# Turning q and k of six batches by VectorE squares and DMA instead of TensorE, in a fused attention and feed-forward kernel

## Chip, cores and metric

One core of a Trainium2 chip (trn2). The metric is device time in microseconds (us) of one execution; lower is better. Every comparison below takes a kernel's fast runs against runs of the kernel before on the same chip in the same rounds. All profiles are of one execution each.

## The reference, cut to what matters

```python
# q, k, v: (8 batches, 8 heads, 576 positions, 64)
scores = scale * np.matmul(q, k.transpose(0, 1, 3, 2))          # scale = 1/8
scores = np.where((rel >= 0) & (rel < 128), scores + bias, -1e9) # ALiBi, window of 128
attn = softmax(scores)
x = (attn @ v).transpose(0, 2, 1, 3).reshape(4608, 512)
h = x @ w_in                                                    # 512 -> 2048
out = np.where(h > 0, h, np.exp(np.minimum(h, 0)) - 1) @ w_out  # 2048 -> 512, ELU
```

For `q @ k.T` TensorE needs q and k with the 64 head dimensions on the partitions, so both have to be turned. The feed-forward part needs x with its 512 features on the partitions, so x is turned as well (tile `xT`).

## The kernel before

The kernel is a list of some 160 steps. Tasks are put into steps by hand with `at(step, f, args)`; each engine executes its own share in the order in which it was issued. Batch b has its attention in steps 16b to 16b+15, the feed-forward part runs beside it. The parts that matter here (cuts are marked `# ...`):

```python
XBAR = 2
QK = [one([128, H, 2, 640], F16, f"QK{i}") for i in range(2)]   # rows 0-63 data, 64-127 bias terms

def load_qk(b, w, h0=0, h1=H):                 # software queue, f32 to f16, 512 KB
    # ...
    nc.gpsimd.dma_start(stq[b][:, w, h0:h1, :, :]..., (q, k)[w][b, h0:h1, 0:512, :]...)

def transposes(b, hp):                         # two heads, q and k, on TensorE
    t = ps_s.tile([128, 2, 2, 4, 2, 32], F16, name="tp", tag="sps")   # the scores' PSUM ring, 2 buffers
    for g in range(2):
        for w in (1, 0):
            for j in range(2):
                nc.tensor.transpose(t[:, g, w, :, j, :], stq[b][...], ident)
    for odd in range(2):                       # evicted by ScalarE (odd hp) or VectorE
        # ...
        if hp % 2: nc.scalar.copy(o, i)
        else:      V.tensor_copy(o, i)

def turn(b, i):                                # x of one block -> xT
    if b >= XBAR:                              # batches 2..7: DMA transpose on SyncE's queue
        # ...
        nc.sync.dma_start_transpose(out=xT[:, :, o:o + n], in_=x[0:n, :])
        return
    # batches 0 and 1: four TensorE transposes into PSUM, one VectorE copy
    # ...

def hidden(t, j):                              # h = x @ w_in for 128x512, then exp and min
    p = hps[t, j] = ps_h.tile([128, 512], F32, name="hp", tag="hp")   # 2 buffers
    # ... nc.tensor.matmul(p[...], w_in_sb[...], xT[...])
    nc.scalar.activation(e, p, AF.Exp)
    nc.gpsimd.tensor_scalar(out=e, in0=e, scalar1=1.0, scalar2=0.0, op0=ALU.min, op1=ALU.max)
# elu(): one VectorE instruction (g) one step later; only it frees the hp buffer

def fill(i):                                   # bias terms, by DMA
    nc.sync.dma_start(QK[i][64:128, :, 0, 0:576], TQ[64:128, :].unsqueeze(1).broadcast_to([64, H, 576]))
    nc.sync.dma_start(QK[i][g_, :, 1, :], TK[g_, :].unsqueeze(1).broadcast_to([32, H, 640]))
# ...
at(s0 + ((5, 9, 10, 13) if b > 1 else ...)[hp], transposes, b + 1, hp)
at(s0 + 10 + 2 * i, load_qk, b + 2, w)         # for b >= 1
```

A hidden block of tokens can start only when their x has landed in `xT`. For batches 2 and 3 that is three steps after `turn`, for batches 4 to 7 seven or more.

The softmax here doesn't subtract the row's maximum and nothing guards it: scores larger than these inputs give would overflow.

Of the kernel before, what the change touches and what calls it, by code (L numbers as in the profile page):

```python
# [9 lines left out]
F16 = mybir.dt.float16  # L10
# [9 lines left out]
def kernel(  # L20
# [9 lines left out]
    nc = tc.nc  # L30
# [34 lines left out]

    QK = [one([128, H, 2, 640], F16, f"QK{i}") for i in range(2)]
    VP = [one([128, 5, H, VW], F16, f"VP{i}") for i in range(2)]
# [5 lines left out]

    stq, stt, vf, vs = {}, {}, {}, {}

# [73 lines left out]
    with tc.manual_schedule():  # L149
# [68 lines left out]
        def zeros():  # L218
            for i in range(2):
                V.memset(QK[i][0:64 + 64 * i, :, 1, 576:640], 0.0)  # L220
                V.memset(VP[i][64:128, 4, :, 0:D], 0.0)
            for e in EX:
                V.memset(e[:, 512:576], 0.0)
# [4 lines left out]
        is96, is97, isx = small("is96"), small("is97"), small("isx")  # L228
        TQ = one([128, 576], F16, "TQ")
        TK = one([128, 640], F16, "TK")  # L230
# [12 lines left out]
        def terms():  # L243

            V.tensor_scalar(out=is96, in0=rowf, scalar1=96.0, scalar2=None, op0=ALU.is_equal)
            V.tensor_scalar(out=is97, in0=rowf, scalar1=97.0, scalar2=None, op0=ALU.is_equal)
            V.tensor_scalar(out=isx, in0=is97, scalar1=-1.0, scalar2=None, op0=ALU.mult)
            V.tensor_scalar(out=pm[r_, :], in0=posi[r_, :], scalar1=float(-MID), scalar2=None,
                            op0=ALU.add)
            V.tensor_scalar(out=TQ[r_, :], in0=pm[r_, :], scalar1=isx[r_, :], scalar2=is96[r_, :],  # L250
                            op0=ALU.mult, op1=ALU.add)
            V.tensor_scalar(out=TK[r_, 0:576], in0=pm[r_, :], scalar1=is96[r_, :],
                            scalar2=is97[r_, :], op0=ALU.mult, op1=ALU.add)
            V.memset(TK[64:128, 576:640], 0.0)

# [8 lines left out]

        def fill(i):
            nc.sync.dma_start(QK[i][64:128, :, 0, 0:576],
                              TQ[64:128, :].unsqueeze(1).broadcast_to([64, H, 576]))
            nc.sync.dma_start(QK[i][g_, :, 1, :], TK[g_, :].unsqueeze(1).broadcast_to([32, H, 640]))

        def fill_k(i):  # L270
            nc.sync.dma_start(QK[i][r_, :, 1, :], QK[1 - i][r_, :, 1, :])

        def k_term(h):
            V.tensor_scalar(out=QK[1][r_, h, 1, :], in0=TK[r_, :],
                            scalar1=8.0 * 2.0 ** (-8.0 * (h + 1) / H), scalar2=None, op0=ALU.mult)

        zeros()
# [8 lines left out]
        def transposes_half(a, hq):  # L286

            if a:
                t = ps_o.tile([128, 4, 2, 2, 2, 32], F16, name="tph", tag="op")
            else:  # L290
                t = ps_s.tile([128, 4, 2, 2, 2, 32], F16, name="tp", tag="sps")
            p = slice(64 * a, 64 * a + 64)
            for w in (1, 0):
                for g in range(4):
                    for j in range(2):
                        nc.tensor.transpose(
                            t[:, g, w, :, j, :],
                            stq[0][p, w, 4 * hq + g, 2 * j:2 * j + 2, :].rearrange("p a d -> p (a d)"),
                            ident[p, p])
            for odd in range(2):  # L300
                r = slice(64 * odd, 64 * odd + 64)
                o = QK[0][0:64, 4 * hq:4 * hq + 4, :, 256 * a:256 * a + 256].rearrange(
                    "p h w (m o i) -> p (h w) m o i", o=2, i=32)[:, :, :, odd, :]
                i = t[r, :, :, :, :, :].rearrange("p h w n a i -> p (h w) (n a) i")
                (nc.scalar.copy if hq else V.tensor_copy)(o, i)

        def transposes(b, hp):
            t = ps_s.tile([128, 2, 2, 4, 2, 32], F16, name="tp", tag="sps")
            for g in range(2):
                for w in (1, 0):  # L310
                    for j in range(2):
                        nc.tensor.transpose(  # L312
                            t[:, g, w, :, j, :],
                            stq[b][:, w, 2 * hp + g, 2 * j:2 * j + 2, :].rearrange("p a d -> p (a d)"),
                            ident)
            for odd in range(2):
                r = slice(64 * odd, 64 * odd + 64)
                o = QK[b % 2][0:64, 2 * hp:2 * hp + 2, :, 0:512].rearrange(
                    "p h w (n a i) -> p (h w) n a i", a=2, i=32)[:, :, :, odd, :]
                i = t[r, :, :, :, :, :].rearrange("p h w n a i -> p (h w) (n a) i")  # L320
                if hp % 2:
                    nc.scalar.copy(o, i)  # L322
                else:
                    V.tensor_copy(o, i)  # L324

        def transposes_tail(b):
            t = ps_s.tile([128, NP, 2, 64], F16, name="tpt", tag="sps")
            for hp in range(NP):
                for w in range(2):
                    nc.tensor.transpose(  # L330
                        t[:, hp, w, :],
                        stt[b][:, w, 2 * hp:2 * hp + 2, :].rearrange("p h d -> p (h d)"),
                        ident[0:64, 0:64])
            for g in range(2):
                r = slice(64 * g, 64 * g + 64)
                V.tensor_copy(
                    QK[b % 2][0:64, :, :, 512:576].rearrange("p (n g) w c -> p n g w c", g=2)[:, :, g, :, :],
                    t[r, :, :, :])

        def scores(b, s):  # L340
# [6 lines left out]
            def mm(o, h, kc, qc, n):  # L347
                nc.tensor.matmul(t[:, o:o + n], qk[0:r, h, 1, kc:kc + 128], qk[0:r, h, 0, qc:qc + n],  # L348
                                 start=b > 0 or o == 0, stop=b > 0)
# [5 lines left out]
            elif i < 4:  # L355
                hs = [2 * p, 2 * p + 1]
                for l in range(2):
                    mm(256 * l, hs[l], 128 * i, 128 * i, 128)
                    mm(256 * l + 128, hs[l], 128 * i - 128, 128 * i, 128)
            else:  # L360
                hs = [4 * p + l for l in range(4)]
                for l in range(4):
                    mm(128 * l, hs[l], 384, 512, 64)
                    mm(128 * l + 64, hs[l], 512, 512, 64)
            if b == 0:
# [161 lines left out]
        for b in range(B):  # L527
# [16 lines left out]
            if b + 1 < B:  # L544
                for hp in range(NP):
                    at(s0 + ((5, 9, 10, 13) if b > 1 else (9, 10, 13, 14) if b else (14, 14, 15, 15))[hp],
                       transposes, b + 1, hp)
                at(s0 + (14 if b else 25), transposes_tail, b + 1)
# [16 lines left out]
        at(9, group_rows)  # L565
        at(10, fill, 1)
        at(10, bands)
        for h in range(H):
            at(11 + h // 2, k_term, h)
        at(22, fill, 0)  # L570
        at(22, fill_k, 0)
        at(9, load_wo, 2, 1)
# [55 lines left out]
```

## Time and profile before

| | |
|---|---|
| time, median of 4 runs | 367.09 us (366.05 to 368.67) |
| TensorE, VectorE, ScalarE, GpSimd busy | 94%, 67%, 57%, 40% |
| one batch of attention in the middle (16 steps) | 36.77 us |
| the same 16 steps with nothing left to turn | 33.69 us |
| moved by DMA | 37.1 MB |

The lines behind it are in the prediction. How to read them: PE is TensorE, PEld its weight loads, DVE VectorE, ACT ScalarE, POOL GpSimd and SP SyncE; L451 is line 451 of the program. A group line has the line of the program, engine, operation, output and input with shapes, the count, then busy us and mean ns of one, then the idle time of the engine just before and what ended it. A chain line has start and length in us. The main instrument of this document is a table of step times: the start of each step's first `hp` matmul, taken from the timeline of TensorE. Where the text says that a step took so long, it is the time from that start in the step before to that start in the step.

### The profile page before, as it was taken

The page shows a single profiled execution, that of the slowest core. Times are in us where ns is not written, and L with a number is a line of the kernel's source. Part 1 is how long each engine was busy: PE and PEld are TensorE (multiplying, and loading weights), DVE is VectorE, ACT ScalarE, POOL GpSimd, SP SyncE. Part 2 cuts the span into 40 slices and gives each one's busy share as a digit, 9 for nine tenths or more (in the row PEclk, how much of TensorE's full clock was granted, in tenths as well). Part 3 has the DMA queues.
Part 4 walks back from the last instruction along what each step waited for, and adds up shares of the span by engine and source line. Part 5 has one row for each costly group of instructions (what it writes and reads, how often), then busy time and mean ns, then how long its engine had stood idle before and what let it go on. Part 6 is the DMA issues. An engine that isn't in the chain of part 4 may idle for free.

```text
span 363.7 us, 9613 instructions
## 1 busy us (share of the span) xinstructions
PE 340.3 (94%) x3790; PEld 251.6 (69%) x3790; DVE 243.5 (67%) x574; ACT 206.7 (57%) x349; POOL 145.7 (40%) x229
## 2 busy tenths in 40 slices
PE   6878997999979999989999999999999999999994
PEld 6766775777647667767777777777777777666651
DVE  6479889678886776666676767776776756634430
ACT  4355583666537655765566665666567565543431
POOL 9146623434314723472346334642433232233320
PEclk9899999999999999999999999999999999999999
DMA  8999999839243973497448934793631222211113
GB/s 114 198 206 119 228 107 183 151 80 155 38 103 89 133 108 84 110 128 110 98 94 127 127 88 100 120 136 82 102 84 45 52 47 45 51 43 47 29 43 73
DMA packets 81948, 37.06 MB, mean 102 GB/s; under 512 B 51952, under 2 KB 77296, under 8 KB 81904
## 3 DMA queue, kind: packets, MB, share of 16 engines
q0 software_dynamic: 34064, 15.40, 35.5%
q1 hardware_dynamic: 47840, 21.06, 25.6%
q8 instruction: 29, 0.48, 0.6%
q14 instruction: 15, 0.12, 0.1%
HBM read 36.70 MB, written 9.44 MB: 127 GB/s over the span
## 4 chain that ended last, share of the span: by engine, by line
PE 65%; DVE 14%; ACT 9%; DMA 7%; issue 3%; POOL 1%; SPq 0%; ACTq 0%; POOLq 0%
PE hp L451 27%; PE op L492 25%; PE sp L348 5%; ACT QK L322 5%; DVE VP L116 4%; DMA vs<-in_v_dram 3%; PE av L394 3%; DVE g L463 3%; ACT EX L372 2%; DVE QK L324 2%; ACT e L455 2%; DVE EX L380 2%; DMA xT<-xn 2%; DMA stq<-in_q_dram 1%; DVE xn L415 1%
## 5 line engine op out<-in xcount | busy, mean ns | idle before, releaser
L456 POOL TENSOR_SCALAR e<-e 128x512 f32<-128x512 f32 x144 | 88.6, 615 | 199.9 <-ACT e L455 199.9
L451 PE MATMUL hp<-xT,wi 128*128 128x256 f16 (+3 forms) x1536 | 150.3, 246 | 8.1 <-DVE g L463 3.6
L451 PEld LDWEIGHTS <-wi 128*128 128x128 f16 x1536 | 121.5, 98 | 49.9 <-DVE g L463 5.5
L455 ACT ACTIVATE e<-hp 128x512 f32<-128x512 f32 x144 | 86.0, 597 | 119.0 <-PE hp L451 110.0
L492 PE MATMUL op<-wo,g 128*128 128x512 f16 x576 | 146.4, 379 | 0.0
L463 DVE SCALAR_TENSOR_TENSOR g<-e,hp 128x512 f16<-128x512 f32 x144 | 98.0, 681 | 23.9 <-POOL e L456 22.7
L380 DVE TENSOR_TENSOR EX<-EX,band 128x512 f16<-128x512 f16 x112 | 49.8, 445 | 57.1 <-ACT EX L372 57.0
L372 ACT ACTIVATE EX<-sp 128x512 f16<-128x512 f32 x128 | 75.9, 593 | 13.3 <-PE sp L368 8.6
L492 PEld LDWEIGHTS <-g 128*128 128x128 f16 x576 | 51.2, 98 | 36.9
L348 PE MATMUL sp<-QK 128*128 128x128 f16 (+3 forms) x576 | 49.8, 213 | 0.0
L394 PE MATMUL av<-VP,EX 128*128 128x65 f16 x576 | 38.6, 193 | 4.3 <-DVE EX L380 2.7
L394 PEld LDWEIGHTS <-EX 128*128 128x128 f16 x576 | 31.6, 98 | 8.7 <-DVE EX L380 4.2
L415 DVE TENSOR_TENSOR xn<-av,rden 128x256 f16<-128x256 f32 x80 | 34.0, 424 | 2.8
L348 PEld LDWEIGHTS <-QK 128*128 128x128 f16 (+1 forms) x576 | 31.3, 97 | 1.0 <-issue 0.2
L496 ACT COPY ob<-op 128x512 f32<-128x512 f32 x36 | 21.1, 586 | 14.3 <-PE op L492 6.4
L322 ACT COPY QK<-tp 64x1024 f16<-64x1024 f16 x28 | 28.1, 1005 | 1.6 <-PE tp L312 1.4
L414 DVE RECIPROCAL rden<-av 128x4 f32<-128x4 f32 x80 | 14.4, 180 | 16.0 <-PE av L394 14.6
L134 POOL TENSOR_SCALAR VP<-vf 128x512 f16<-128x512 f32 (+1 forms) x25 | 19.5, 779 | 2.7 <-DMA vf<-in_v_dram 2.7
L324 DVE COPY QK<-tp 64x1024 f16<-64x1024 f16 x28 | 19.2, 684 | 1.1 <-PE tp L312 0.8
L312 PE MATMUL tp<-ident,stq 128*128 128x128 f16 x224 | 17.1, 219 | 2.3 <-ACT QK L322 1.0
L312 PEld LDWEIGHTS <-stq 128*128 128x128 f16 x224 | 13.8, 98 | 3.4 <-issue 3.2
L116 DVE COPY VP<-vs 32x512 f16<-32x512 f16 x48 | 14.9, 310 | 1.3 <-DMA vs<-in_v_dram 0.5
(70 smaller groups left out, 118.5 us busy)
## 6 DMA issues: line engine op xcount, KB each, us to landing
out_dram<-ob SPq DMA_DIRECT2D x128, 64.0 KB, 1.7
vf<-in_v_dram SPq DMA_DIRECT2D x80, 64.0 KB, 2.3
stq<-in_k_dram POOLq DMA_DIRECT2D x7, 512.0 KB, 6.4
stq<-in_q_dram POOLq DMA_DIRECT2D x7, 512.0 KB, 7.5
wi<-in_moe_w_in_dram POOLq DMA_DIRECT2D x4, 512.0 KB, 13.8
wo<-in_moe_w_out_dram POOLq DMA_DIRECT2D x4, 512.0 KB, 15.1
QK<-TQ SPq DMA_DIRECT2D x2, 576.0 KB, 8.0
vs<-in_v_dram POOLq DMA_DIRECT2D x2, 512.0 KB, 9.9
```

The source lines that it names most:

```text
L312: nc.tensor.transpose(t[:, g, w, :, j, :], stq[b][:, w, 2 * hp + g, 2 * j:2 * j + 2, :].rearrange("p a d -> p (a d)"), ident)
L322: nc.scalar.copy(o, i)
L348: nc.tensor.matmul(t[:, o:o + n], qk[0:r, h, 1, kc:kc + 128], qk[0:r, h, 0, qc:qc + n], start=b > 0 or o == 0, stop=b > 0)
L372: nc.scalar.activation(e[:, 0:512], t, AF.Exp, scale=0.125)
L380: V.tensor_tensor(out=e, in0=e, in1=band[:, c:c + n].unsqueeze(1).broadcast_to([128, 512 // n, n]), op=ALU.min)
L394: nc.tensor.matmul(a[:, l, :], e[:, c:c + 128], vp[:, n, h, 0:D + 1], start=st, stop=sp)
L415: V.tensor_tensor(out=xnt[b, i][:, 4 * half:4 * half + 4, :], in0=a[:, :, 0:D], in1=r.unsqueeze(2).broadcast_to([128, 4, D]), op=ALU.mult)
L451: nc.tensor.matmul(p[:, l * w + u0:l * w + u1], w_in_sb[:, c, fc * 128:(fc + 1) * 128], xT[:, c, x0:x0 + u1 - u0], start=(c == 0), stop=(c ...
L455: nc.scalar.activation(e, p, AF.Exp)
L456: nc.gpsimd.tensor_scalar(out=e, in0=e, scalar1=1.0, scalar2=0.0, op0=ALU.min, op1=ALU.max)
L463: V.scalar_tensor_tensor(out=gs[t][:, f0:f0 + nf, c0:c0 + w], in0=sh(es.pop((t, j))), scalar=1.0, in1=sh(hps.pop((t, j))), op0=ALU.subtrac ...
L492: nc.tensor.matmul(ops[t], gs[t][:, fc, ts * 128:(ts + 1) * 128], w_out_sb[:, fc, :], start=(fc == 0), stop=(fc == NFC - 1))
```

## The change

Its intent: TensorE is 94% busy, and turning q and k costs it 192 matmuls in batches 2 to 7, plus evictions that hold the scores' PSUM ring. VectorE can transpose 32x32 squares from SBUF to SBUF. The squares then lie on the wrong partitions, so DMA carries them over; to give the DMA runs of 2 KB the tile QK is stored block by block. The bias terms (`fill`) would need many small runs in that layout, so engines write them for one buffer and one DMA copies the other.

```diff
-    QK = [one([128, H, 2, 640], F16, f"QK{i}") for i in range(2)]
+    QK = [one([128, 2, 5, H, 128], F16, f"QK{i}") for i in range(2)]
...
-        def fill(i):        # two broadcast DMAs for each buffer
+        def fill_q(n):
+            nc.scalar.copy(QK[1][64:128, 0, n, :, :], TQ[64:128, 128*n:128*n+128]...broadcast)
+        def fill_k(n):
+            V.tensor_copy(QK[1][g_, 1, n, :, :], TK[g_, 128*n:128*n+128]...broadcast)
+        def fill_other():
+            nc.sync.dma_start(QK[0][64:128], QK[1][64:128])
...
+        def squares(b, n):   # 128x512, sixteen columns of 32x32 squares
+            if b not in tt:
+                tt[b] = stage.tile([128, 2, 2, H, 4, 32], F16, name="tt", tag="tt", bufs=1)
+            w, dh, hs = 1 - n // 4, n // 2 % 2, slice(4 * (n % 2), 4 * (n % 2) + 4)
+            V.transpose(out=tt[b][:, w, dh, hs, :, :]..., in_=stq[b][:, w, hs, :, 32*dh:32*dh+32]...)
+        def collect(b, n):   # 128 KB, 64 runs of 2 KB, 32 partitions to 32 others
+            i, dh = n // 2, n % 2
+            nc.sync.dma_start(QK[b % 2][32*dh:32*dh+32, :, i, :, :]..., tt[b][32*i:32*i+32, :, dh, ...]...)
...
-                    at(s0 + ((5, 9, 10, 13) if b > 1 else ...)[hp], transposes, b + 1, hp)
+                for n in range(8 if b else 0):
+                    at(s0 + (n if b > 1 else 6 + n // 2), squares, b + 1, n)
+                    at(s0 + (8 if b > 1 else 10) + n // 2, collect, b + 1, n)
```

Left out: the index changes that follow from the new layout in `scores`, `put`, `k_term`, the tail and the zeroing. Batch 1 keeps its TensorE turns.

More of the change, by code (lines that the diff above doesn't have):

```diff
@@ L71 @@
     xT = one([128, 4, RING], F16, "xT")
-    stq, stt, vf, vs = {}, {}, {}, {}
+    stq, stt, vf, vs, tt = {}, {}, {}, {}, {}
     def load_qk(b, w, h0=0, h1=H):
@@ L219, in zeros @@
             for i in range(2):
-                V.memset(QK[i][0:64 + 64 * i, :, 1, 576:640], 0.0)
+                V.memset(QK[i][0:64 + 64 * i, 1, 4, :, 64:128], 0.0)
                 V.memset(VP[i][64:128, 4, :, 0:D], 0.0)
@@ L228 @@
         is96, is97, isx = small("is96"), small("is97"), small("isx")
-        TQ = one([128, 576], F16, "TQ")
+        TQ = one([128, 640], F16, "TQ")
         TK = one([128, 640], F16, "TK")
@@ L249, in terms @@
                             op0=ALU.add)
-            V.tensor_scalar(out=TQ[r_, :], in0=pm[r_, :], scalar1=isx[r_, :], scalar2=is96[r_, :],
+            V.tensor_scalar(out=TQ[r_, 0:576], in0=pm[r_, :], scalar1=isx[r_, :], scalar2=is96[r_, :],
                             op0=ALU.mult, op1=ALU.add)
@@ L253, in terms @@
                             scalar2=is97[r_, :], op0=ALU.mult, op1=ALU.add)
-            V.memset(TK[64:128, 576:640], 0.0)
+            for t in (TQ, TK):
+                V.memset(t[64:128, 576:640], 0.0)
         def group_rows():
@@ L263, in group_rows @@
                 V.tensor_copy(t[g_, 256:512], t[g_, 0:256])
-        def fill(i):
-            nc.sync.dma_start(QK[i][64:128, :, 0, 0:576],
-                              TQ[64:128, :].unsqueeze(1).broadcast_to([64, H, 576]))
-            nc.sync.dma_start(QK[i][g_, :, 1, :], TK[g_, :].unsqueeze(1).broadcast_to([32, H, 640]))
-        def fill_k(i):
-            nc.sync.dma_start(QK[i][r_, :, 1, :], QK[1 - i][r_, :, 1, :])
+        def fill_q(n):
+            nc.scalar.copy(QK[1][64:128, 0, n, :, :],
+                           TQ[64:128, 128 * n:128 * n + 128].unsqueeze(1).broadcast_to([64, H, 128]))
+        def fill_k(n):
+            V.tensor_copy(QK[1][g_, 1, n, :, :],
+                          TK[g_, 128 * n:128 * n + 128].unsqueeze(1).broadcast_to([32, H, 128]))
         def k_term(h):
-            V.tensor_scalar(out=QK[1][r_, h, 1, :], in0=TK[r_, :],
+            V.tensor_scalar(out=QK[1][r_, 1, :, h, :], in0=TK[r_, :].rearrange("p (n c) -> p n c", c=128),
                             scalar1=8.0 * 2.0 ** (-8.0 * (h + 1) / H), scalar2=None, op0=ALU.mult)
+        def fill_other():
+            nc.sync.dma_start(QK[0][64:128], QK[1][64:128])
         zeros()
@@ L288, in transposes_half @@
             if a:
-                t = ps_o.tile([128, 4, 2, 2, 2, 32], F16, name="tph", tag="op")
+                t = ps_o.tile([128, 2, 2, 4, 2, 32], F16, name="tph", tag="op")
             else:
-                t = ps_s.tile([128, 4, 2, 2, 2, 32], F16, name="tp", tag="sps")
+                t = ps_s.tile([128, 2, 2, 4, 2, 32], F16, name="tp", tag="sps")
             p = slice(64 * a, 64 * a + 64)
@@ L296, in transposes_half, with put @@
                         nc.tensor.transpose(
-                            t[:, g, w, :, j, :],
+                            t[:, w, :, g, j, :],
                             stq[0][p, w, 4 * hq + g, 2 * j:2 * j + 2, :].rearrange("p a d -> p (a d)"),
                             ident[p, p])
+            put(t, QK[0][0:64, :, 2 * a:2 * a + 2, 4 * hq:4 * hq + 4, :], hq)
+        def put(t, o, by_act):
             for odd in range(2):
-                r = slice(64 * odd, 64 * odd + 64)
-                o = QK[0][0:64, 4 * hq:4 * hq + 4, :, 256 * a:256 * a + 256].rearrange(
-                    "p h w (m o i) -> p (h w) m o i", o=2, i=32)[:, :, :, odd, :]
-                i = t[r, :, :, :, :, :].rearrange("p h w n a i -> p (h w) (n a) i")
-                (nc.scalar.copy if hq else V.tensor_copy)(o, i)
+                (nc.scalar.copy if by_act else V.tensor_copy)(
+                    o.rearrange("p w n h (a o i) -> p w n h a o i", o=2, i=32)[:, :, :, :, :, odd, :]
+                    .rearrange("p w n h a i -> p w n (h a) i"),
+                    t[64 * odd:64 * odd + 64].rearrange("p w n h a i -> p w n (h a) i"))
         def transposes(b, hp):
-            t = ps_s.tile([128, 2, 2, 4, 2, 32], F16, name="tp", tag="sps")
+            t = ps_s.tile([128, 2, 4, 2, 2, 32], F16, name="tp", tag="sps")
             for g in range(2):
@@ L312, in transposes @@
                         nc.tensor.transpose(
-                            t[:, g, w, :, j, :],
+                            t[:, w, :, g, j, :],
                             stq[b][:, w, 2 * hp + g, 2 * j:2 * j + 2, :].rearrange("p a d -> p (a d)"),
                             ident)
-            for odd in range(2):
-                r = slice(64 * odd, 64 * odd + 64)
-                o = QK[b % 2][0:64, 2 * hp:2 * hp + 2, :, 0:512].rearrange(
-                    "p h w (n a i) -> p (h w) n a i", a=2, i=32)[:, :, :, odd, :]
-                i = t[r, :, :, :, :, :].rearrange("p h w n a i -> p (h w) (n a) i")
-                if hp % 2:
-                    nc.scalar.copy(o, i)
-                else:
-                    V.tensor_copy(o, i)
+            put(t, QK[b % 2][0:64, :, 0:4, 2 * hp:2 * hp + 2, :], hp % 2)
+        def squares(b, n):
+            if b not in tt:
+                tt[b] = stage.tile([128, 2, 2, H, 4, 32], F16, name="tt", tag="tt", bufs=1)
+            w, dh, hs = 1 - n // 4, n // 2 % 2, slice(4 * (n % 2), 4 * (n % 2) + 4)
+            V.transpose(out=tt[b][:, w, dh, hs, :, :].rearrange("p h j i -> p (h j) i"),
+                        in_=stq[b][:, w, hs, :, 32 * dh:32 * dh + 32].rearrange("p h j d -> p (h j) d"))
+        def collect(b, n):
+            i, dh = n // 2, n % 2
+            nc.sync.dma_start(
+                QK[b % 2][32 * dh:32 * dh + 32, :, i, :, :].rearrange("p w h c -> p w (h c)"),
+                tt[b][32 * i:32 * i + 32, :, dh, :, :, :].rearrange("p w h j i -> p w (h j i)"))
         def transposes_tail(b):
-            t = ps_s.tile([128, NP, 2, 64], F16, name="tpt", tag="sps")
+            t = ps_s.tile([128, 2, NP, 64], F16, name="tpt", tag="sps")
             for hp in range(NP):
@@ L330, in transposes_tail @@
                     nc.tensor.transpose(
-                        t[:, hp, w, :],
+                        t[:, w, hp, :],
                         stt[b][:, w, 2 * hp:2 * hp + 2, :].rearrange("p h d -> p (h d)"),
@@ L334, in transposes_tail @@
             for g in range(2):
-                r = slice(64 * g, 64 * g + 64)
                 V.tensor_copy(
-                    QK[b % 2][0:64, :, :, 512:576].rearrange("p (n g) w c -> p n g w c", g=2)[:, :, g, :, :],
-                    t[r, :, :, :])
+                    QK[b % 2][0:64, :, 4, :, 0:64].rearrange("p w (n g) c -> p w n g c", g=2)[:, :, :, g, :],
+                    t[64 * g:64 * g + 64, :, :, :])
         def scores(b, s):
@@ L347, in mm @@
             def mm(o, h, kc, qc, n):
-                nc.tensor.matmul(t[:, o:o + n], qk[0:r, h, 1, kc:kc + 128], qk[0:r, h, 0, qc:qc + n],
+                nc.tensor.matmul(t[:, o:o + n], qk[0:r, 1, kc, h, :], qk[0:r, 0, qc, h, 0:n],
                                  start=b > 0 or o == 0, stop=b > 0)
@@ L357, in scores @@
                 for l in range(2):
-                    mm(256 * l, hs[l], 128 * i, 128 * i, 128)
-                    mm(256 * l + 128, hs[l], 128 * i - 128, 128 * i, 128)
+                    mm(256 * l, hs[l], i, i, 128)
+                    mm(256 * l + 128, hs[l], i - 1, i, 128)
             else:
@@ L362, in scores @@
                 for l in range(4):
-                    mm(128 * l, hs[l], 384, 512, 64)
-                    mm(128 * l + 64, hs[l], 512, 512, 64)
+                    mm(128 * l, hs[l], 3, 4, 64)
+                    mm(128 * l + 64, hs[l], 4, 4, 64)
             if b == 0:
@@ L544 @@
             if b + 1 < B:
-                for hp in range(NP):
-                    at(s0 + ((5, 9, 10, 13) if b > 1 else (9, 10, 13, 14) if b else (14, 14, 15, 15))[hp],
-                       transposes, b + 1, hp)
+                for hp in range(NP if b == 0 else 0):
+                    at((14, 14, 15, 15)[hp], transposes, 1, hp)
+                for n in range(8 if b else 0):
+                    at(s0 + (n if b > 1 else 6 + n // 2), squares, b + 1, n)
+                    at(s0 + (8 if b > 1 else 10) + n // 2, collect, b + 1, n)
                 at(s0 + (14 if b else 25), transposes_tail, b + 1)
@@ L565 @@
         at(9, group_rows)
-        at(10, fill, 1)
+        for n in range(5):
+            at(10 + n, fill_q, n)
+            at(10 + n, fill_k, n)
         at(10, bands)
@@ L569 @@
             at(11 + h // 2, k_term, h)
-        at(22, fill, 0)
-        at(22, fill_k, 0)
+        at(20, fill_other)
         at(9, load_wo, 2, 1)
```

## The prediction

> **What bounds the kernel now.** I read the page first (busy shares, chain of waits, groups), then the chain in order of time, then the timeline step by step. The kernel runs in some 160 steps; a full one has one hidden block (L451), the scores and values of one bank (L348, L394) and four output products (L492).
>
> ```profile
> PE 340.3 (94%) x3790; PEld 251.6 (69%) x3790; DVE 243.5 (67%) x574; ACT 206.7 (57%) x349; POOL 145.7 (40%) x229
> PE 65%; DVE 14%; ACT 9%; DMA 7%; issue 3%; POOL 1%; SPq 0%; ACTq 0%; POOLq 0%
> L322 ACT COPY QK<-tp 64x1024 f16<-64x1024 f16 x28 | 28.1, 1005 | 1.6 <-PE tp L312 1.4
> L324 DVE COPY QK<-tp 64x1024 f16<-64x1024 f16 x28 | 19.2, 684 | 1.1 <-PE tp L312 0.8
> L312 PE MATMUL tp<-ident,stq 128*128 128x128 f16 x224 | 17.1, 219 | 2.3 <-ACT QK L322 1.0 <-ACT EX L372 0.6 <-DVE QK L336 0.6
> L116 DVE COPY VP<-vs 32x512 f16<-32x512 f16 x48 | 14.9, 310 | 1.3 <-DMA vs<-in_v_dram 0.5
> ```
>
> TensorE is the bound on the whole, but a third of the chain lies elsewhere. The timeline of batch 4 (engine lines of 189 to 196 us) shows what a turn of two heads costs beside its own eight matmuls:
>
> ```profile
> 189.26 0.61 PE L312 MATMUL tp<-ident,stq 128*128 128x128 f16 x8
> 190.09 2.02 ACT L322 COPY QK<-tp 64x1024 f16<-64x1024 f16 x2
> 192.13 0.60 ACT L455 ACTIVATE e<-hp 128x512 f32<-128x512 f32 x1
> 192.16 0.61 PE L312 MATMUL tp<-ident,stq 128*128 128x128 f16 x8 [0.21 <-ACT QK L322]
> 193.62 1.38 DVE L324 COPY QK<-tp 64x1024 f16<-64x1024 f16 x2
> 195.04 0.69 DVE L463 SCALAR_TENSOR_TENSOR g<-e,hp 128x512 f16<-128x512 f32 x1
> 195.78 1.03 PE L451 MATMUL hp<-xT,wi 128*128 128x256 f16 x8
> ```
>
> The two ScalarE evictions hold the score buffer, so the next turn waits; then the two VectorE evictions push g back to 195.04, and the hidden block, whose next LDWEIGHTS had been ready at 195.34, starts only at 195.78. Two earlier stretches are bound by VectorE, not TensorE. In the chain in order of time, around step 17:
>
> ```profile
> 53.27 0.49 DVE VP L116
> 55.02 0.69 DVE g L463
> 56.03 0.42 DVE xn L415
> 58.34 0.69 DVE g L463
> ```
>
> and by the windows view (stretch, engine sums, clock, DMA) of the start to batch 2, a batch in the middle and one with nothing left to turn:
>
> ```profile
> 10.00:52.00 42.00, 36.36 (x533) 29.38 (x532) 32.36 (x89) 23.16 (x35) 16.62 (x25) 0.98 1.23 179
> 100.00:139.00 39.00, 35.11 (x377) 25.34 (x375) 28.16 (x67) 23.52 (x40) 15.61 (x26) 1.00 0.66 106
> 212.70:249.50 36.80, 36.33 (x381) 26.75 (x380) 25.99 (x59) 23.58 (x40) 16.64 (x25) 1.00 0.67 111
> 286.20:320.00 33.80, 33.80 (x343) 24.48 (x341) 20.73 (x46) 19.00 (x34) 9.96 (x17) 1.00 0.23 52
> ```
>
> **What the Trainium skill says.** (1) "VectorE: DVE Perf Modes", The three transpose paths: VectorE turns 32x32 blocks only, 128x128 bf16 in 311 ns; "Vector Engine (DVE) Microarchitecture Reference", 3.8: the array sustains one element per cycle per lane. At the first page's 0.96 GHz a square of 512 columns is then an estimate of 311 + 384/0.96 = 711 ns. No VectorE transpose is in the trace, but its one-element-a-cycle groups agree in slope: xn of 256 elements takes 424 ns, g of 512 takes 681. (2) The same table gives TensorE 390 ns; here a run of eight takes 0.45 us on the chain, 56 ns each, so what the trace shows decides. (3) "DMA: Bandwidth & Descriptors", Anatomy of one DMA: about 2.0 us fixed and the bytes over 436 GB/s. The page of before has 64 KB landing in 1.7 to 2.4 us, which agrees; for a 128 KB collect I estimate 2.3 to 3 us. (4) SKILL, "Trainium Kernel Development and Optimization", Key Constraints: all queues run on the same 16 DMA engines. Agrees: one xT transpose took 5.5 us on the chain (158.30) where the median is 2.4, while 512 KB loads of q and k were in flight.
>
> **The change, part by part.**
>
> *Batches 3 to 7 (turned during batches 2 to 6).* Removed per batch: 32 matmuls (4 x 0.45 = 1.8 us of TensorE, all on the path), 4 ScalarE evictions (4.0 us) and 4 VectorE evictions (2.7 us). A batch takes 36.77 us now: the ScalarE evictions that start the second pair recur at 190.09, 226.86, 263.63. Sixteen steps with nothing to turn take 33.69 (hidden blocks of 279.10 and 312.79 on the chain); the tail turn, which stays, adds about 0.45. So 36.77 - 34.14 = 2.6 us per batch are to be had: 1.8 of matmuls and 0.8 of waits like those shown. Added: 8 squares of about 0.66 us back to back (busy times overlap by some 0.05 to 0.08 us: g is 0.68 busy, 0.60 on the chain), one in each of steps 0 to 7. A step without normalize costs VectorE 0.44 (cut) + 0.61 (g) + 0.66 = 1.7 us against a step of 2.08; with normalize (steps 0, 1, 2, 4, 6) 0.55 more, 2.26. So VectorE runs 0.17 over in each of those and 0.36 under in steps 3, 5, 7. The cut has 0.32 us of slack before its values (ends 179.70, values at 180.02), g some 0.26 once a square is ahead of it. Three heavy steps in a row overrun by 0.5, so some 0.3 us reaches TensorE. Net gain 2.3 us for batches 3 to 6: 9.2 us.
>
> *During batch 2.* The same 2.6 is to be had, but steps 32 to 35 also place v (4 copies of 0.29 each), and VectorE is without a gap from 94.69 to 105.7. Four squares come straight on top: 2.6 us. With the rest I take +0.4.
>
> *During batch 1 (for batch 2).* Squares two a step in steps 22 to 25: VectorE then needs 2.93 + 2.73 + 2.93 + 3.23 = 11.8 us (with a tail eviction of 0.85) where TensorE needs 9.1; less 0.5 slack, 2.2 lost. Removed: 1.8 of matmuls and 1.4 of waits in steps 25 to 32 (21.37 us now against 18.2 counted from its parts). Net +0.7 with 0.3 of them kept.
>
> *The fill of batch 0.* Two DMA broadcasts go; VectorE gets 5 copies of 32x1024, ScalarE 5 of 64x1024, in steps 10 to 14. From 34.7 to 43 us VectorE has 0.2 us of idle time, so its copies count in full: a copy of 32x512 took 285 ns (median of L116), one of 32x256 took 210, so 1024 is about 0.41, 2.0 in all. ScalarE's are 1.0 us each by L322; four fit in its gaps, the one in step 14 meets two evictions (2.0) and costs perhaps 0.8. Back comes the 0.5 us wait for v at 50.46. Net -2.3.
>
> *The collects.* 48 DMAs of 128 KB, 6.3 MB beside 37: two a step in steps 8 to 11, first needed at step 16, so 8 us for 3: hidden. SP needs some 0.45 us to issue one (four stores take 1.73), which fits. But they share engines with xT: block 2 of batches 2 and 3 is turned at steps 43 and 59 and needed three steps later, and the latter already stalls TensorE 1.1 us. I allow -1.0.
>
> Sum: 9.2 + 0.4 + 0.7 - 2.3 - 1.0 = 7.0 us; 366.4 - 7.0 = 359.4. Loads, tails, the output and the end do not change.
>
> **Rivals.**
> *VectorE becomes the bound.* For: 243.5 us busy, and 48 squares at 0.7 less 24 evictions at 0.684, plus fills, add 19 us; in steps 0 to 7 I have it at 98% (16.4 of 16.7 us). Every 0.1 us more per square would add about 0.6 us per batch. Against: most of a batch has a free VectorE microsecond per step. If squares take 0.85 us, gains shrink to about 1.2 per batch and batches 1 and 2 turn to losses: 364 to 366.
> *The early part costs nothing.* For: less DMA before 50 us lets v and weights land sooner, and ScalarE is only 55% busy there. Against: the gapless VectorE. Then 355 to 357.
> *The collects hold up xT.* For: the 5.5 us transpose. Against: batches 4 to 7 have seven steps between a turn and its use. Two stalls of 2 us more: 362 to 363.
>
> **Range and chances.** The gain of 9.2 is the surest, give or take 1.5; batch 0 may be -4 or -0.5; batches 1 and 2 together -2 to +3; xT 0 to -3. Added not quite in step, that is 354.5 to 364.5. The 2% line is 359.1, nearly on the middle; no change is likely if a little more of the squares shows: faster 0.46, same 0.49, slower 0.05.
>
> **What would show it right or wrong.** Squares of 0.68 to 0.72 us in the groups; batches 4 to 6 repeating every 34.3 to 34.7 us; no wait of TensorE for L322 or L324 after batch 1; stretch 10 to 52 us some 2 us longer with VectorE gapless; waits on VectorE in steps 22 to 25 and 32 to 35; collects landing in 3 us and no wait of the scores on them; one or two xT waits of 1 to 2 us. The prediction falls if squares take over 0.8 us, if the fill is free, or if SP's queue holds xT back.

## The result

The changed kernel took **385.49 us** (median of 4 runs, 383.18 to 388.31) against 367.09 for the kernel before: a ratio of 1.0501, 95% interval 1.0419 to 1.0583, so 5% slower. Ratios here are the mean time of one kernel's fast runs over that of the other's in the same rounds, so not quite the ratio of the medians quoted. Executions over 1.5% slower than the fastest of the same kernel are left out of the means. Predicted were 359.4 us and a range of 354.5 to 364.5.

From the changed kernel's page (busy shares; chain; the group of the squares; the collects with their KB and median us to landing):

```profile
PE 338.4 (88%) x3598; PEld 246.7 (64%) x3598; DVE 257.9 (67%) x604; ACT 189.4 (49%) x330; POOL 145.2 (38%) x229
PE 63%; DMA 15%; DVE 14%; ACT 3%; issue 2%; SPq 1%; POOL 0%; ACTq 0%; POOLq 0%; DVEq 0%
L331 DVE STREAM_TRANSPOSE tt<-stq 128x512 f16<-128x512 f16 x48 | 33.2, 698 | 5.0 <-DMA out_dram<-ob 4.4
QK<-tt SPq DMA_DIRECT2D x48, 128.0 KB, 5.0
```

ScalarE's 9% share of the chain fell to 3%, but DMA's rose from 7 to 15%. A square takes 698 ns, as foreseen. A collect takes 5.0 us in the median, not the 2.3 to 3 foreseen. The view of who waited for whom (us in total, times, longest), first of the kernel before, then of the changed one:

```profile
PE hp L451 <- DVE g L463: 3.6, 6, 0.9
PE hp L451 <- DMA xT<-xn: 1.4, 2, 1.1
```

```profile
PE hp L465 <- DMA xT<-xn: 16.4, 2, 8.3
PE hp L465 <- DVE g L477: 9.6, 9, 2.3
DVE tt L331 <- DMA out_dram<-ob: 4.4, 2, 2.7
```

TensorE stood 16.4 us in two waits for `xT`. The step table says where the time went; a positive number is time lost against the kernel before:

| steps | changed minus before, us | what stands there |
|---|---|---|
| start to 9 | +1.2 | 0.6 of it at step 4 already (see below) |
| 9 to 16 | +2.3 | the fill on VectorE and ScalarE |
| 16 to 33 | -1.5 | squares two a step, TensorE turns gone |
| 33 to 39 | +5.7 | squares beside the placing of v; then a slow clock |
| 39 to 45 | -1.5 | turns gone |
| 45 to 48 | +8.4 | first wait for xT, slow clock behind it |
| 48 to 61 | -2.0 | turns gone |
| 61 to 64 | +9.2 | second wait for xT, slow clock |
| 64 to 80 | -2.8 | turns gone; every step of 66 to 78 takes 2.08 us |
| 80 to 82 | +1.4 | a square waits |
| 82 to 95 | -2.7 | turns gone |
| 95 to 99 | +4.6 | a square waits, slow clock |
| 99 to 149 | -2.7 | turns gone, then nothing |
| sum | +19.6 | profiled spans 363.7 and 383.6 |

The start to step 4 is not a finding: it lay between 16.0 and 18.1 us over all the profiles, of either layout.

The second of the two waits, in the chain in order of time (start, length, what), before and after:

```profile
158.30 5.50 DMA xT<-xn
163.85 1.05 PE hp L451 x8
```

```profile
169.57 6.54 DMA QK<-tt
176.17 6.99 DMA xT<-xn
183.29 1.87 PE hp L465 x8
186.34 1.82 PE op L506 x4
```

The chain names the collect of 169.57, but its landing is only the last piece of a longer hold-up. The block's x was ready at 168.31 (end of `xn` on VectorE). SyncE issues in order and had four collects, a load of v and four stores to issue first, until 175.44; the last 0.7 us it waited for that collect to land, because in the built program each DMA signals its landing on one of eight counters, and the next DMA on the same counter waits for it. So x lay 7.9 us before SyncE issued the transpose at 176.17, against 3.7 us in the kernel before. Then xT itself takes 7 us, and after 8.3 us without work TensorE is slow: the same eight matmuls take 1.87 us instead of 1.05. The windows view of the changed kernel from that point (stretch and its length, engines, then granted clock, DMA, GB/s):

```profile
183.20:187.20 4.00, 3.91 (x31) 2.72 (x32) 1.28 (x4) 1.19 (x2) 0.61 (x1) 0.50 0.22 20
187.20:191.20 4.00, 4.00 (x38) 2.67 (x37) 2.47 (x7) 1.72 (x3) 0.61 (x1) 0.82 0.23 57
191.20:200.00 8.80, 8.80 (x93) 6.53 (x91) 7.72 (x18) 4.97 (x9) 2.45 (x4) 1.00 0.38 82
```

The granted clock is 0.50 for four microseconds, 0.82 in the mean of the next four and whole after that. The Trainium skill has this in "TensorE: Matmul & The Clock Gate", Part 1: half the clock after an idle window of some 3.4 us, full clock after as long a busy one; the trace agrees: TensorE stopped at 175.0, the clock was halved from 178.4 and whole again from 188.6, some 5 us after work was back. It makes such a gap dearer than its length: step 62 to 63 took 4.66 us against 2.54.

The waiting square at step 80, from VectorE's timeline:

```profile
226.75 0.42 DVE L394 TENSOR_TENSOR EX<-EX,band 128x512 f16<-128x512 f16 x1 [0.27 <-ACT EX L386]
228.86 0.71 DVE L331 STREAM_TRANSPOSE tt<-stq 128x512 f16<-128x512 f16 x1 [1.69 <-DMA out_dram<-ob]
```

The profile names a store of the output. A square has no business with it. In the built program this first square of a batch waits for seven counters of SyncE's DMA queue and for one load of k; stores and collects share the counters, so the view's name for the wait can be another DMA's. Landing times tell which it was, in the DMA view of short stretches (KB, us to landing): first the one at 213.5 to 214.0 us, then 220.7 to 222.5:

```profile
stq<-in_k_dram POOLq DMA_DIRECT2D x1, 512.0 KB, 8.7
QK<-tt SPq DMA_DIRECT2D x1, 128.0 KB, 2.4
```

```profile
QK<-tt SPq DMA_DIRECT2D x2, 128.0 KB, 7.1
```

The load of k was issued at 213.76 and so in by 222.5; the last collect was issued at 221.75 and landed at 228.68. The trace also holds the waits of VectorE's sequencer, which the timeline leaves out: it stood from 226.93 to 228.72 at a pair of counters, one of them the counter of this collect, and the square started at 228.86. So the square waited for the collect: `tt` has one buffer. The same lines show more: a collect issued before the loads of q and k took 2.4 us, one issued while they were under way 7.1.

### The profile page after: what moved, and what is told of

Same layout as the page of the kernel before. It is cut to its first block, busy times and chain, and to the rows that moved or that the text cites. A ratio compares the mean times of both kernels' runs of the same rounds, so it can differ in the third digit from the quotient of the medians.

```text
span 383.6 us, 9352 instructions
## 1 busy us (share of the span) xinstructions
PE 338.4 (88%) x3598; PEld 246.7 (64%) x3598; DVE 257.9 (67%) x604; ACT 189.4 (49%) x330; POOL 145.2 (38%) x229
## 4 chain that ended last, share of the span: by engine, by line
PE 63%; DMA 15%; DVE 14%; ACT 3%; issue 2%; SPq 1%; POOL 0%; ACTq 0%; POOLq 0%; DVEq 0%
PE hp L465 27%; PE op L506 24%; PE sp L362 6%; DMA QK<-tt 5%; DMA xT<-xn 4%; DMA out_dram<-ob 4%; DVE VP L117 4%; PE av L408 4%; DVE g L477 3%; DVE tt L331 2%; DMA stq<-in_q_dram 1%; ACT EX L386 1%; DVE xn L429 1%; DVE EX L394 1%; PE spare L519 1%
## 5 line engine op out<-in xcount | busy, mean ns | idle before, releaser
L465 PE MATMUL hp<-xT,wi 128*128 128x256 f16 (+3 forms) x1536 | 156.4, 252 | 27.3 <-DMA xT<-xn 16.4
L465 PEld LDWEIGHTS <-wi 128*128 128x128 f16 x1536 | 124.9, 100 | 71.0 <-issue 25.1
L506 PE MATMUL op<-wo,g 128*128 128x512 f16 x576 | 149.2, 385 | 0.0
L477 DVE SCALAR_TENSOR_TENSOR g<-e,hp 128x512 f16<-128x512 f32 x144 | 96.6, 671 | 24.6 <-POOL e L470 23.8
L408 PEld LDWEIGHTS <-EX 128*128 128x128 f16 x576 | 32.8, 100 | 12.4 <-DVE EX L394 5.4
L331 DVE STREAM_TRANSPOSE tt<-stq 128x512 f16<-128x512 f16 x48 | 33.2, 698 | 5.0 <-DMA out_dram<-ob 4.4
L117 DVE COPY VP<-vs 32x512 f16<-32x512 f16 x48 | 16.7, 348 | 0.7
L519 PE MATMUL spare<-ident 128*128 128x128 f16 x94 | 9.0, 272 | 1.6 <-DVE ident L176 1.6
L519 PEld LDWEIGHTS <-ident 128*128 128x128 f16 x94 | 8.1, 126 | 1.7 <-DVE ident L176 1.6
L310 ACT COPY QK<-tp 64x1024 f16<-64x1024 f16 x6 | 6.0, 1007 | 5.9 <-PE tp L301 4.4
```

The source lines that it names most:

```text
L117: V.tensor_copy(VP[b % 2][32 * j:32 * j + 32, n, :, 0:D], vs[b][32 * n:32 * n + 32, :, j, :])
L331: V.transpose(out=tt[b][:, w, dh, hs, :, :].rearrange("p h j i -> p (h j) i"), in_=stq[b][:, w, hs, :, 32 * dh:32 * dh + 32].rearrange("p ...
L408: nc.tensor.matmul(a[:, l, :], e[:, c:c + 128], vp[:, n, h, 0:D + 1], start=st, stop=sp)
L465: nc.tensor.matmul(p[:, l * w + u0:l * w + u1], w_in_sb[:, c, fc * 128:(fc + 1) * 128], xT[:, c, x0:x0 + u1 - u0], start=(c == 0), stop=(c ...
L477: V.scalar_tensor_tensor(out=gs[t][:, f0:f0 + nf, c0:c0 + w], in0=sh(es.pop((t, j))), scalar=1.0, in1=sh(hps.pop((t, j))), op0=ALU.subtrac ...
L506: nc.tensor.matmul(ops[t], gs[t][:, fc, ts * 128:(ts + 1) * 128], w_out_sb[:, fc, :], start=(fc == 0), stop=(fc == NFC - 1))
```

## The experiments

Theory A: the collects' DMA costs the time. They meet the 512 KB loads of q and k on the shared DMA engines, so `xT` and the collects themselves land late. Theory B, the rival of the prediction: VectorE's 33 us of squares have made it the bound. Theory C: not the engines but SyncE's queue is at fault, which issues collects, stores and xT in order. All twelve kernels ran with 3 rounds, and each was within the comparison's tolerance.

### e1: no collects

```diff
-                    at(s0 + (8 if b > 1 else 10) + n // 2, collect, b + 1, n)
```

> The changed kernel without its 48 collects; the result is wrong on purpose (q and k of batches 2 to 7 stay those of an earlier batch). Theory A, the collects' DMA is what costs: both long xT waits (8.1 and 8.3 us) and the waits of the squares at steps 32, 80 and 96 go, TensorE keeps its clock; what stays is the fill of batch 0 (+3.6 us) and the gapless VectorE of steps 32 to 35 (+2.6), against 2.75 us gained per batch: 357 to 362 us. Theory B, VectorE's 33 us of squares are what costs: still over 378 us.

Measured: 361.73 us, ratio 0.986 (0.9804 to 0.9915). The result, wrong, passed the comparison all the same: with inputs of this size the scores are around 0.01, so stale q and k hardly move the softmax. That comparison therefore does not vouch for q and k in any kernel here. Squares still took 697 ns and all 48 were there, so **theory B falls**: 24 us of the changed kernel's time went with the collects alone. VectorE does bound one stretch, as the prediction had it: without any collect steps 33 to 39 still lost 4.6 us against before, and in the chain of this run VectorE's work stands there from 97.2 to 107.4 us. One xT wait of 2.9 us stayed at step 62:

```profile
PE hp L465 <- DMA xT<-xn: 3.1, 2, 2.9
```

### e2: the collects on ScalarE's queue

```diff
-            nc.sync.dma_start(QK[b % 2][32 * dh...
+            nc.scalar.dma_start(QK[b % 2][32 * dh...
```

> The collects issued by ScalarE instead of SyncE, nothing else. If the hold-up is SP's order (0.6 us to issue each collect, xT behind them in one queue), the xT waits of TensorE fall under 1.5 us each and the time to 364 to 371 us. If it is the DMA engines that all queues share, the waits stay at 5 us or more and the time at 380 to 390.

Measured: 399.46 us, ratio 1.0872 (1.0805 to 1.0939): slower than both cases expected. Steps 46 and 62 took 11.3 and 8.3 us. That does not refute theory C, because SyncE was not freed: the eight landing counters are shared by the DMAs of SyncE and ScalarE, and SyncE's stores now waited for collects that ScalarE had issued. From the waits of SyncE (with `--engine SP`):

```profile
SPq L512 <- DMA QK<-tt: 16.6, 8, 4.4
```

The xT of steps 46 and 62 was issued even later after its x was ready than in the changed kernel (7.0 and 10.0 us against 4.6 and 7.9). At step 46 the transfer was slow as well, 8.7 us; that transfers meet whichever engine issues them is what the Trainium skill says in "DMA: Bandwidth & Descriptors", Issuing engines are not separate DMA queues. At step 62 it landed 2.5 us after its issue, and TensorE stood there for `g`, behind GpSimd, which waited 7.4 us before a cast of v. New waits came at steps 78 and 94 (9.5 and 9.0 us). In the chain around step 78 and in GpSimd's timeline:

```profile
213.40 9.34 DMA vf<-in_v_dram
```

```profile
222.96 0.62 POOL L135 TENSOR_SCALAR VP<-vf 128x512 f16<-128x512 f32 x1 [8.57 <-DMA vf<-in_v_dram]
```

A load of v took 9.34 us; GpSimd stood in order before its cast for 8.57 us, and behind that cast stood the feed-forward's `e`. So moving the collects delayed more work, and the run does not tell queue from engines.

### e3: the kernel before, with copies of the collects' size

48 DMAs from `stq` into a tile QX that nobody reads, in the collects' steps. For want of space half of them write to partitions 64 to 127.

```diff
+        def collect(b, n):
+            nc.sync.dma_start(QX[p:p + 32, :, i % 2, :], stq[b][32 * i:32 * i + 32, :, 4 * dh:4 * dh + 4, :, :]...)
+                for n in range(8 if b else 0):
+                    at(s0 + (8 if b > 1 else 10) + n // 2, collect, b + 1, n)
```

> The kernel before with 48 DMAs of the collects' sizes, partitions and steps into a tile that nobody reads; its own TensorE turns stay. Theory A: the xT waits of step 46 and above all of step 62 (1.1 us in before) grow to 4 us or more each, time 374 to 382 us. Theory B: within 1% of before, 366 to 370.

Measured: 377.91 us, ratio 1.0301 (1.0237 to 1.0365). Theory A, as expected:

```profile
PE hp L460 <- DMA xT<-xn: 11.2, 2, 5.7
```

Steps 46 and 62 took 7.56 and 8.22 us against 2.16 and 3.81 in before; apart from slow steps right behind these two, none changed much. So the copies alone, with TensorE still turning q and k and not one square on VectorE, make most of the two losses.

### e4: xT of batches 2 and 3 by TensorE

```diff
-    XBAR = 2
+    XBAR = 4
```

> The changed kernel with xT of batches 2 and 3 turned by TensorE too (as batches 0 and 1 are), so no xT DMA has to land within three steps. Costs 40 matmuls (2.2 us) and 10 VectorE evictions of 0.42. Theory A: both long waits and the slow clock behind them go, the waits of the squares for collects stay: 368 to 374 us. Theory B: 385 or more, VectorE having more to do.

Measured: 364.72 us, ratio 0.9929 (0.9883 to 0.9974): better than expected. The two long waits are gone (steps 46 and 62: 1.23 and 2.11 us). The waits of squares remain (2.9 us named for stores, 0.6 for collects). This becomes the base of most of the next runs. They ran on another chip; the intervals of their ratios overlap with this one's, so what e6, e7 and e8 show rests on their step times.

### e5: the loads of q and k ten steps earlier

On the changed kernel, xT by DMA as it was.

```diff
-                    at(s0 + 10 + 2 * i, load_qk, b + 2, w)
-                    at(s0 + 11 + 2 * i, load_tail, b + 2, w)
+                    at(s0 + (0 if b > 1 else 10) + 2 * i, load_qk, b + 2, w)
+                    at(s0 + (1 if b > 1 else 11) + 2 * i, load_tail, b + 2, w)
```

> The changed kernel with the 512 KB loads of q and k, and their tails, of batches 4 to 7 issued ten steps earlier in the same batch, so that they no longer meet the collects. If xT is late because collects and loads meet on the shared engines, the waits at steps 46 and 62 fall from 8 us to under 2 and the slow clock after them goes: 366 to 373 us. If the collects alone (1 MB in four steps ahead of xT) do it, the waits stay at 5 us or more and the time at 379 to 386.

Measured: 370.06 us, ratio 1.0071 (1.0022 to 1.012), where the changed kernel had 1.0501. From its waits and its page:

```profile
PE hp L465 <- DMA xT<-xn: 6.6, 3, 3.9
QK<-tt SPq DMA_DIRECT2D x48, 128.0 KB, 2.5
```

The collects' median fell from 5.0 to 2.5 us without a change to them. **Their meeting with the loads is what makes the collects late**, and it lengthens xT's transfers. It is not all of xT's delay: 6.6 us of its waits are left, 3.9 of them now at step 55, behind the loads' new place. The traces of the runs so far split that delay for the two blocks of x that steps 46 and 62 need (from the end of `xn` to the issue on SyncE, and from there to the landing, us):

| | step 46: to issue, to landing | step 62: to issue, to landing |
|---|---|---|
| before | 1.1, 6.4 | 3.7, 5.5 |
| changed | 4.6, 9.2 | 7.9, 7.0 |
| e1, no collects | 0.3, 5.5 | 2.9, 6.6 |
| e2, collects by ScalarE | 7.0, 8.7 | 10.0, 2.5 |
| e3, before with copies | 5.4, 7.6 | 5.9, 7.7 |
| e5, loads early | 4.3, 2.5 | 5.5, 2.5 |

The time before the issue is SyncE's order, with its waits for landing counters in it. So theory C holds in part. Against e1 the collects made xT 8.0 us later at step 46, 4.3 of it before the issue; at step 62 it was 5.4 us, 5.0 of it before the issue. With the loads away (e5) the transfers took 2.5 us and most of the time before the issue stayed.

### e6: squares and collects of batches 4 to 7 two steps later

On e4.

```diff
-  squares at s0 + n,     collects at s0 + 8 + n // 2     (b > 2)
+  squares at s0 + 2 + n, collects at s0 + 10 + n // 2    (b > 2)
```

> As e4_xt_pe (xT of batches 2 and 3 by TensorE), with the squares and collects of batches 4 to 7 two steps later. If the squares of steps 80 and 96 waited for the tile tt, which the last collects of the batch before were still reading, VectorE's waits before squares (2.9 us) go there and steps 82 and 98 fall to 2.1 us each: 1.5 to 2.5 us under e4_xt_pe, 362 to 363.5. If they waited for a load of q or k, nothing changes.

Measured: 362.19 us, ratio 0.9871 (0.983 to 0.9912). Steps 82 and 98 fell from 2.87 and 3.66 us in e4 to 2.09 each. VectorE's waits before squares fell from 3.5 to 0.7 us. Alone this would fit a late load as well; with the landing times and the sequencer's wait above and e8 below, the one buffer of `tt` is the cause.

### e7: the fill by DMA

On e4; ten DMAs with runs of 256 bytes.

```diff
-            nc.scalar.copy(QK[1][64:128, 0, n, :, :], TQ...)
+            nc.sync.dma_start(QK[1][64:128, 0, n, :, :], TQ...)
-            V.tensor_copy(QK[1][g_, 1, n, :, :], TK...)
+            nc.sync.dma_start(QK[1][g_, 1, n, :, :], TK...)
```

> As e4_xt_pe, with the fill of batch 0 by DMA again (ten DMAs of 256-byte runs into the new layout) instead of VectorE and ScalarE copies. The prediction put the fill's copies at 2.3 us (steps 9 to 16 took 2.3 longer): if so 362 to 363; if the small runs hold up the load of v instead, no gain or 1 to 3 us longer.

Measured: 362.46 us, ratio 0.9868 (0.9837 to 0.99). Steps 9 to 16 took 19.8 us against 21.4 in e4, 21.5 in the changed kernel and 19.2 before: the fill's copies cost 1.6 us in these steps (2.3 between the two medians), near the 2.3 predicted.

### e8: squares of batch 3 in steps 36 to 43

On e4; its collects in steps 44 to 47.

> As e4_xt_pe, with the squares of batch 3 in steps 36 to 43 instead of 32 to 39, so that none meets the placing of v, and its collects in steps 44 to 47. If the four squares in VectorE's gapless stretch count in full (2.6 us in the prediction), 361.5 to 363 us; if TensorE's stalls there have another cause, 364 to 365.

Measured: 364.17 us, ratio 0.9908 (0.986 to 0.9957): a miss. Steps 33 to 39 did fall from 20.7 to 16.7 us. But step 50 took 5.25 us, because the first square of batch 4, at step 48, now came right behind the collects of batch 3:

```profile
DVE tt L331 <- DMA QK<-tt: 3.5, 1, 3.5
```

Here the profile names the collect itself: the wait for `tt`, moved to where the move put it.

### c1, c2, c3: the mends together, and b4, a control

c1 is e4, e6, e7 and e8 in one (squares of batches 4 to 7 begin two steps later, so e8's new wait has room). c2 adds e5's early loads. c3 is c2 with xT of batches 2 and 3 by DMA. b4 is the kernel before with `XBAR = 4`. They were run on another chip.

```diff
-    XBAR = 2
+    XBAR = 4                                   # c1, c2, b4; not c3
-  squares at s0 + n,                           collects at s0 + 8 + n // 2    (b > 1)
+  squares at s0 + (2 + n if b > 2 else 4 + n), collects at s0 + (10 if b > 2 else 12) + n // 2
   # fill_q, fill_k as in e7; load_qk, load_tail as in e5 (c2, c3)
```

> The mends together: xT of batches 2 and 3 by TensorE, the fill by DMA, the squares of batch 3 in steps 36 to 43 and of batches 4 to 7 in steps 2 to 9 with their collects behind. If the four causes add up (e6 362.2, less 2.3 of the fill, less the 3.9 that steps 33 to 39 gave in e8): 355.5 to 358 us, over 2% faster than before. If they overlap: 359 to 361.

> As c1_mended, with the loads of q and k ten steps earlier as in e5_loads_early. xT is no longer in danger and the squares are already late enough, so no more than 1 us either way against c1: 355 to 358.

> As c2, but xT of batches 2 and 3 by DMA again. TensorE saves 2.2 us of matmuls and VectorE ten evictions; against that stand xT waits, 6.6 us in e5_loads_early. With the collects of batch 3 now at steps 44 to 47, behind the xT of step 43, I expect 1 to 4 us of them: 355 to 360.

> The kernel before with xT of batches 2 and 3 by TensorE: a control for the mend. It loses its own 1.4 us of xT waits and pays 2.2 us of matmuls and VectorE evictions: 366 to 369 us, so that the mended versions' gain is not the mend's own.

| | median us | ratio to before | 95% |
|---|---|---|---|
| c1 | 355.10 | 0.9671 | 0.9619 to 0.9723 |
| c2 | 353.05 | 0.9625 | 0.9578 to 0.9673 |
| c3 | 364.14 (363.86 without the slow run) | 0.9872 | 0.9796 to 0.9948 |
| b4 | 368.77 | 1.0024 | 0.9977 to 1.0071 |

c2 is 3.75% faster than the kernel before, which the mend of xT alone does not help (b4). So the idea of the change is good; the transfers around it had to be moved. From c2's page:

```profile
PE 331.1 (94%) x3638; PEld 243.8 (69%) x3638; DVE 259.0 (74%) x609; ACT 185.1 (53%) x325; POOL 145.0 (41%) x229
QK<-tt SPq DMA_DIRECT2D x48, 128.0 KB, 2.4
```

VectorE has more to do than in the slow kernel and TensorE is busy for 94% again. Steps 66 to 82 take 34.0 us where before took 36.8. c1 and c2 came a little under what was expected, c2 by 2 us; the two intervals overlap, so what the early loads add to c1 is not settled (in the one profile of each, steps 33 to 39 took 18.1 us in c1 and 15.2 in c2, as in before). What early loads alone would give the kernel before was not run. c3 is a miss, and whether it gains the 2% is unclear, its interval reaching over 0.98: two xT waits of 8.2 us in all stay even with early loads, and the time varies (359.5 to 364.4 us in the fast runs, the profile being of the fastest). In this program's traffic a slack of three steps was too short for xT's DMA.

## Why the prediction was wrong

**Where it held.** The squares: 711 ns estimated, 698 measured. The gain per batch from the freed TensorE: 2.3 predicted, 2.7 to 2.8 measured in the undisturbed stretches (64 to 80, 82 to 95, 99 to 112), where steps beside a square took 2.08 us with no stall at all. The fill: 2.3 predicted, 2.3 measured in steps 9 to 16 (1.6 of it gone in e7). Steps 16 to 33: 0.7 predicted to be gained, 1.5 measured; only the sign was right, since the 2.2 us that VectorE was to cost in steps 22 to 25 did not come (step 24 lost 0.4). VectorE as the bound of the whole, the first rival, did not come about. That e1, without the DMA, took 361.73 us and not some 358.4 (the sum without its 1.0 for xT) is what the terms other than the DMA were off by, with an xT wait of 2.9 us in it.

**The step that failed** is "The collects": "two a step in steps 8 to 11, first needed at step 16, so 8 us for 3: hidden", with "-1.0" for xT and "SP needs some 0.45 us to issue one ... which fits". It asked when the collects are needed and not what else is on the engines while they fly and what stands behind them in SyncE's order. The terms that were mis-sized or missing:

- xT: 1.0 us allowed, 17.6 lost in steps 45 to 48 and 61 to 64, slow clock included (e1, e3 and e4: gone without collects or without xT's DMA, there with copies alone). The third rival named this mechanism and put it at two stalls of 2 us more; they were of 7 each, and each cost another 1 to 2 us of slow clock. More than half of what the collects added to xT's delay lay before its issue, in SyncE's order (the table in e5): a collect took 0.6 us to issue, not 0.45, and x lay 4.6 and 7.9 us until its transpose was issued. The prediction's own sign of being wrong, "if SP's queue holds xT back", came true. It had in hand the 5.5 us transpose at 158.30, its cause (the loads of q and k, steps 58 and 60) and the collects' steps (56 to 59), and did not add them up.
- A collect: 2.3 to 3 us estimated from its size, 2.4 when it met no load and 7.1 when it did (e5: 2.5 in the median once the loads had moved).
- Missing: that `tt` has one buffer, so that a late collect holds the next batch's first square, and through VectorE's order g and the hidden block. Steps 80 to 82 and 95 to 99 lost 6.0 us by it, slow clock included; in steps 33 to 39 it was a small part, 1.1 us (5.7 lost in the changed kernel, 4.6 in e1 without collects).

A smaller one: for steps 32 to 35 the four squares' 2.6 us were right in kind and too small. Without collects the stretch lost 4.6 us (e1), and moving the squares away gave 4.0 (e8). In e1 the granted clock fell there too, to 0.69 in the mean of step 39; how much of the difference is slow clock was not measured on its own.

**What stays open.** The traces split xT's delay into time before the issue and time in flight, but no run took SyncE's order away by itself: in e2 the shared landing counters held SyncE up, and ScalarE and the loads of v had other things to wait for. Issuing xT ahead of the collects was not tried. Whether it matters that collects write to 64 partitions only was not tried; e3 wrote half of its copies to the other 64 and had the waits.

## What to carry to other kernels

A transfer that is needed late is not therefore free: list what else is in flight in the same steps, what the issuing engine has to issue first, and what small, urgent DMA has the least slack there; an existing 5.5 us instance of a 2.4 us transfer is a warning that the stretch is full. When work moves from an engine to DMA, look at buffers that a DMA reads (`tt`), since a late reader stalls the next writer. And when a change loses, take its suspected cost away by itself first: e1 showed in one run that the idea was sound and the transfers were not.

## What the Trainium skill lacked or had wrong

- "DMA: Bandwidth & Descriptors", Anatomy of one DMA: the section's 2.0 us plus bytes over 436 GB/s is given for the software queue of GpSimd. It also fits a collect of 128 KB on SyncE's queue that is alone (an estimate of 2.3 us from it, 2.4 measured). There is no figure for a small DMA that meets software-queue loads: 7.1 us for the same collect, and 9.2 us at worst for an xT transpose whose median is 2.5.
- The same page, Issuing engines are not separate DMA queues, gives issue time as the only thing that a second issuing engine changes. In this program it changed more, for the worse: 399 us against 385, SyncE's stores waiting 16.6 us for collects that ScalarE had issued, since both use the same landing counters. That is of the program, not of the chip; the page has no word on it.
- "VectorE: DVE Perf Modes", The three transpose paths, times 128x128 only. 128x512 of f16 took 0.698 us with a source of 32-element runs, near the estimate of 711 ns.
- "TensorE: Matmul & The Clock Gate", Part 1, speaks of an idle window and gives no figure for how little work counts as idle. Here a whole gap of 8.3 us halved the clock, but so did, where a square waited in the changed kernel, a stretch of 3.4 us in which TensorE was busy for 1.2 us and never idle for more than 2.3:

```profile
263.70:267.14 3.44, 1.22 (x13) 0.48 (x9) 1.28 (x3) 1.08 (x2) 0.61 (x1) 1.00 1.35 212
267.14:270.56 3.42, 3.35 (x19) 2.30 (x20) 2.75 (x9) 1.19 (x2) 0.61 (x1) 0.50 0.23 43
```
